# Values and float64 words loaded in pairs, combine weights turned by float32r products, four more unread products

## The chip, the cores and the metric

The kernel runs on one core of a Trainium2 chip. The metric is the device time of one execution in microseconds; a lower one is better. Several executions are timed, and one more is recorded by the hardware profiler, which gives the rows below.

## What is computed

Three layers follow one another on 4608 tokens of 512 channels, in float32, and the last one has weights in float64.

```python
# 1. attention inside chunks of 64 positions, 8 batches x 8 heads, head width 64
scores = q_c @ k_c.T / 8;  attn = softmax(scores);  x = attn @ v_c
# 2. soft mixture of 8 experts, 4 slots each (32 slots)
logits = x @ phi                                   # 4608 x 32
d = softmax over tokens(logits);  slot_in = d.T @ x  # 32 x 512
h = relu(slot_in[e] @ w1[e]);  slot_out[e] = h @ w2[e]
c = softmax over slots(logits);  y = c @ slot_out    # "combine weights" c
# 3. SoLU layer, w_in and w_out are float64
h = y @ w_in;  s = h * softmax(h);  out = layernorm(s) * g_ln @ w_out
```

## The kernel before, in words

The tokens are 36 tiles of 128. A first loop takes one tile per step: scores S (line 254), their row maximum (L263), the subtraction (L269), exp (L275), a transpose of the attention weights (L405), the product with the values (L280), the division by the row sums, a transpose of the result (L414) and its slot logits. Softmax over tokens is kept running over blocks of four tiles.

Beside each step the loop converts one chunk of the float64 weights of the last layer. A chunk is 128 x 256 words of 64 bits, loaded as pairs of 32-bit words into a tile `raw`; ScalarE makes a mask value of the high words (`sq`, L204) and shifts the low words (`t`, L208), VectorE takes high words twice (`u`, L211; `a`, L221), GpSimd puts the pieces together. Step i converts chunk i - 2 and issues, at the name `raw`, the load of chunk i + 2. The 32 chunks have four `raw` tiles. Values come one tile at a time into `vall` (three places, L180), queries and keys into three buffers (L175), and at the name `W` the next of 64 expert weight tiles of 512 KB is loaded if the table `PACE` allows it and one of 24 ring buffers is free (L128).

The order of everything is written by hand. `STEP` holds four lines, one for step i mod 4 = 0 to 3, and each name in a line issues its instructions in that order. `FIRST` orders the first loads. After step 33 `ORDER` names every operation once; a program checks that what an operation needs has gone before. Engines work through their own instructions in order. All loads go out on SyncE, in order too; each waits for its buffer and for one of eight places in the queue, and the place is free when the load eight before it has landed.

When the loop ends, buffers that it no longer needs are given to the weight loads (`homes`, `own`): the `raw` tiles, the query buffers, the values and so on. After the last tile a short chain makes the slot inputs: logits of the last block, maximum over tokens (`mnl`, `mb`), exp, the slot sums (`sl`, L681), their scaling (`siT`). Then TensorE takes the expert products in the order of the weight tiles (L933, L970, L984; last the tiles `wc48` to `wc63`). Between them stand the turns of the combine weights, `ct0` to `ct8`: for four tiles of tokens the weights are split into a high and a low float32r part (`cc`), transposed by TensorE (`combine_t`, L916) and copied to `c4T`. The names `id0` to `id3` are products of the identity with itself into PSUM that nobody reads (L643). From 191 us on the last layer runs, bound to products L1307 and L1389.

Of the kernel before, what the change touches and what calls it, by code (L numbers as in the profile page):

```python
# [9 lines left out]
F32 = mybir.dt.float32  # L10
F32R = mybir.dt.float32r
# [9 lines left out]
NB = 9  # L21
RING = 24
NRAW = 32
# [6 lines left out]
S a m t x xT u mT qk rz PT mx v xTe sub PTe W rc add mul raw exp xm mn d sq de  # L30
S a x u v m qk rz sl mx t W raw rc z xT sub xTe PT PTe add xm acc mul sq exp
m t S u a x qk rz xT mx W sub xTe PT rc acc v PTe add LT xm mul sq raw exp lte
t m a S x u L tm v mx xT add qk PT lall rz mul xTe sub rc raw PTe W sq xm exp
"""
# [8 lines left out]
GATE = dict()  # L43
FIRST = "raw0 qk0 qk1 v0 qk2 v1 cs raw1 g phi raw2 raw3"
ORDER = """
cq1 cq2 cq3 cq4 cq5 cq6 cq7 S34 loadw xT31 PT33 xtev31 x32 mx34 rz32 LT31 sub34 ev32 own_c S35 ptev33 lte7 mx35 exp34
sub350 PT34 x33 ptev34 xT32 exp350 L7 rz33 xtev32 own_q sub351 x34 ev33 exp351 PT350 id0 rz34 ptev0 xT33 PT351 LT32 lall7
tm7 x350 ptev1 ev34 x351 xtev33 xT34 LT33 id1 xtev34 own_v rz35 rc35 ev350 ev351 LT34 id2 xT350 px lte8 xT351 xtev350 xtev351
L8 own_p LT35 tm8 mT8 lte83 Ls mn8 L83 lall83 hz1 mnl own_t mb lall8 cm0 id3 d7 d8 mc de7 al sl71 de8 sl70 own_x hz0 z8
sl80 zacc8 sl81 zt acc80 acc81 zr si0 si1 siT open2 cm1 w1_000 cme w1_001 cz0 rl00 w1_010 cms2 cms6 px2 cms3 ht00 he00  # L50
# [17 lines left out]
def soft_moe_kernel(ctx: ExitStack, tc, qkT, v1, w12, w64, phi, g_ln, cst, out):  # L68
# [95 lines left out]
    for i in range(3):  # L164
        nc.vector.memset(qk[i][:, 0, :], 0.0)
        nc.gpsimd.memset(qk[i][:, 2, :], 0.0)
    vall = cvb.tile([128, 3, 520], F32, name="vall")
    XT = cvb.tile([128, 4, 4, 128], F32, name="xt_b")
# [9 lines left out]
    def load_v(t):  # L178
        if t < NT:
            gated("v", nc.sync.dma_start(out=vall[:, t % 3, :], in_=v1[t]))  # L180

    raw_t = {}

    def load_raw(c):
        if c < NRAW:
            raw_t[c] = cvp.tile([128, 256, 2], U32, tag="raw", name="raw", bufs=4)
            gated("raw", nc.sync.dma_start(out=raw_t[c].rearrange("p n t -> p (n t)"), in_=w64[c].bitcast(U32)))

# [88 lines left out]
    def x_mm(i, x, pt, g):  # L277
        for a in range(2):
            for c in range(2):
                nc.tensor.matmul(  # L280
                    x[ts(c, 64), a, ts(g, 65)],
                    pt[ts(a, 64), ts(c, 64)],
                    vall[ts(a, 64), i % 3, ts(2 * g + c, 65)],
                    start=True, stop=True, tile_position=(64 * a, 64 * c),
                )
# [183 lines left out]
    def step_ops(i):  # L469
# [20 lines left out]
        def W():  # L490
# [4 lines left out]
            u=(cvc, lambda: cv_u(c)), m=(cvc, lambda: cv_m(c)), a=(cvc, lambda: cv_a(c)), add=(cvc, lambda: cv_s(c)),  # L495
            mul=(cvc, lambda: cv_w(c)), raw=(cvc, lambda: load_raw(c + 4)),
            sq=(True, lambda: cv_sq(cstep.get(i + 1, NRAW))), t=(True, lambda: cv_t(cstep.get(i + 1, NRAW))),
# [75 lines left out]

    op("x32")(lambda: (pe_x(n - 3), load_v(n)))
    op("x33", "ptev33 ev32")(lambda: pe_x(n - 2))
# [70 lines left out]
    op("id1", "LT33 id0")(lambda: idle(lt_t[last][:, 3, :], 2))  # L646
    op("id2", "LT34 id1")(lambda: idle(lt_t[last][:, 3, :], 2))
    op("id3", "cm0 mnl ev34 id2")(lambda: idle(sx[:, 0, 256:384], 2))

# [109 lines left out]

    def raw_pair():  # L760
        return [
            cvp.tile([128, 256, 2], U32, tag="raw", name="w_raw", bufs=4).rearrange("p n t -> p (n t)").bitcast(F32)
            for _ in range(2)
        ]

# [7 lines left out]
    homes = dict(  # L773
        raw0=raw_pair, raw1=lambda: raw_pair(),
        conv=lambda: [conv.bitcast(F32).rearrange("p (k a) n -> p k (a n)", k=2)],
        v=lambda: [va[:, 0:1024].rearrange("p (a b) -> p a b", a=2)],
        pt=pt_pair, p=p_pair,
        xt0=lambda: [XT[:, 0:2].rearrange("p t g n -> p t (g n)")], xt1=lambda: [XT[:, 2:4].rearrange("p t g n -> p t (g n)")],
# [14 lines left out]
    op("own_q", "S35 own_c")(lambda: own("qk2"))  # L793
    op("own_v", "x34 x351 own_q")(lambda: own("v", "pt"))
    op("own_p", "own_v x351 PT34")(lambda: own("p"))
# [82 lines left out]

    e1 = ps2 = soT = cz = mx = late = c4T = e3c = ps3 = None
    op("open2", "siT")(open_2)  # L880
# [27 lines left out]
    def combine_t(b):  # L908
        cc = cc_t[b].bitcast(F32)
        if ps3 is None:  # L910
            t = ps2.tile([128, 4, 128], F32, tag="c", name="c_ps")
        else:
            t = ps3.tile([128, 4, 128], F32, tag="uhT_ps", name="c_ps", bufs=1)
        T["c", b] = t
        for k in range(4):
            nc.tensor.transpose(t[:, k, :], cc[:, k].rearrange("p r s -> p (r s)"), ident)  # L916

# [173 lines left out]
    def open_late():  # L1091
        nonlocal late, c4T, e3c
# [401 lines left out]
```

## Time and profile before

| | us |
|---|---|
| runs | 408.98, 413.80, 414.86 (median 413.8) |
| profiled execution | 411.12 |
| its span, first to last instruction | 409.3 |
| TensorE busy / VectorE / ScalarE / GpSimd in the span | 388.1 / 312.7 / 224.5 / 200.3 |
| moved by DMA | 99.2 MB, mean 242 GB/s |

Busy time of TensorE is modelled, so that 95% does not say that it works at its peak. What bounds a stretch is read from what its engines waited for, and from the GB/s of that stretch. [...]

### The profile page before, as it was taken

The page shows a single profiled execution, that of the slowest core. Times are in us where ns is not written, and L with a number is a line of the kernel's source. Part 1 is how long each engine was busy: PE and PEld are TensorE (multiplying, and loading weights), DVE is VectorE, ACT ScalarE, POOL GpSimd, SP SyncE. Part 2 cuts the span into 40 slices and gives each one's busy share as a digit, 9 for nine tenths or more (in the row PEclk, how much of TensorE's full clock was granted, in tenths as well). Part 3 has the DMA queues.
Part 4 walks back from the last instruction along what each step waited for, and adds up shares of the span by engine and source line. Part 5 has one row for each costly group of instructions (what it writes and reads, how often), then busy time and mean ns, then how long its engine had stood idle before and what let it go on. Part 6 is the DMA issues. An engine that isn't in the chain of part 4 may idle for free. (4 is left out here: it accounts for less than half of the span.)

```text
span 409.3 us, 10399 instructions
## 1 busy us (share of the span) xinstructions
PE 388.1 (95%) x3953; PEld 223.0 (54%) x3953; DVE 312.7 (76%) x777; ACT 224.5 (55%) x471; POOL 200.3 (49%) x198
## 2 busy tenths in 40 slices
PE   3998998999999899989999999999999999999996
PEld 2776776877787652345544444444444444444445
DVE  2688888889887447683898989998888888888840
ACT  2477877777785412232557775555455555455521
POOL 1477776677778228240013345555454444544430
PEclk9999999999999989999999999999999999999999
DMA  7999999999999999994055767777556666587671
GB/s 264 307 377 400 389 370 389 395 398 388 400 381 386 398 382 385 408 408 134 2 95 134 132 137 158 157 157 158 135 132 153 147 134 132 134 148 152 131 156 51
DMA packets 106337, 99.20 MB, mean 242 GB/s; under 512 B 78640, under 2 KB 79280, under 8 KB 106288
## 3 DMA queue, kind: packets, MB, share of 16 engines
q1 hardware_dynamic: 106288, 98.55, 78.0%
q8 instruction: 31, 0.51, 0.5%
q14 instruction: 18, 0.15, 0.1%
HBM read 70.60 MB, written 9.44 MB: 196 GB/s over the span
## 5 line engine op out<-in xcount | busy, mean ns | idle before, releaser
L1190 POOL TENSOR_SCALAR uh<-u,sc 128x1024 f16<-128x1024 f32 (+1 forms) x35 | 66.1, 1889 | 50.5 <-issue 37.6
L1389 PEld LDWEIGHTS <-uhT 128*128 128x128 f16 x560 | 52.2, 98 | 68.4 <-issue 8.9
L1389 PE MATMUL o_ps<-xb,uhT 128*128 128x512 f16 x280 | 66.6, 380 | 0.7 <-DMA uhT<-uh 0.7
L1389 PE MATMUL o_ps<-xb,ulT 128*128 128x512 f16 x280 | 66.3, 379 | 0.1
L1389 PE MATMUL o_ps<-wo,uhT 128*128 128x512 f16 x280 | 66.1, 379 | 0.0
L1318 ACT ACTIVATE e<-h_ps,nm 128x1024 f32<-128x1024 f32 x34 | 37.8, 1113 | 44.9 <-DVE nm L1312 44.9
L1206 ACT ACTIVATE e<-u,nmean 128x1024 f32<-128x1024 f32 x35 | 40.1, 1147 | 28.5 <-DVE nmean L1205 28.4
L254 PE MATMUL s_ps<-qk 128*64 128x128 f32 x576 | 42.4, 292 | 9.2 <-DMA qk<-in_qkT 6.7
L1356 POOL TENSOR_TENSOR a<-a,mhalf 128x1 f32<-128x1 f32 x36 | 21.8, 606 | 56.3 <-DVE a L1373 43.4
L1312 DVE TENSOR_REDUCE nm<-h_ps 128x1 f32<-128x1024 f32 x34 | 41.5, 1221 | 10.2 <-PE h_ps L1307 10.2
L1181 DVE SCALAR_TENSOR_TENSOR u<-h_ps,e 128x1024 f32<-128x1024 f32 x35 | 42.8, 1224 | 6.6 <-ACT e L1318 6.6
L1389 PEld LDWEIGHTS <-ulT 128*128 128x128 f16 x280 | 27.2, 98 | 33.5 <-DMA ulT<-ul 0.6
L1366 DVE SCALAR_TENSOR_TENSOR ul<-u,sc,uh 128x1024 f16<-128x1024 f32 x35 | 45.4, 1296 | 0.0
L254 PEld LDWEIGHTS s_ps<-qk 128*64 128x64 f32 x576 | 33.4, 145 | 16.3 <-issue 10.0
L263 DVE TENSOR_REDUCE mx<-s_ps 128x8 f32<-128x512 f32 x36 | 24.7, 686 | 13.0 <-PE s_ps L254 12.8
L396 ACT ACTIVATE xt_b<-xt_ps 128x512 f32<-128x512 f32 (+1 forms) x37 | 21.6, 586 | 16.3 <-PE xt_ps L414 15.3
L217 POOL TENSOR_SCALAR conv<-conv 128x256 f32<-128x256 f32 x16 | 17.4, 1090 | 23.7 <-ACT conv L204 23.1
L1407 ACT ACTIVATE ob<-o_ps,a 128x512 f32<-128x512 f32 x35 | 23.8, 680 | 9.4 <-PE o_ps L1389 8.0
L1307 PE MATMUL h_ps<-s,c4T 128*128 128x512 f32 x68 | 27.5, 488 | 0.0
L280 PE MATMUL x_ps<-vall,pt 64*64 64x65 f32 x1088 | 24.4, 227 | 1.9 <-issue 0.8
L275 ACT ACTIVATE p<-p 128x512 f32<-128x512 f32 x35 | 21.8, 621 | 7.0 <-DVE p L269 7.0
L217 POOL TENSOR_SCALAR conv<-conv,g_sb 128x256 f32<-128x256 f32 x16 | 19.0, 1185 | 12.2 <-ACT conv L204 12.2
(234 smaller groups left out, 643.2 us busy)
## 6 DMA issues: line engine op xcount, KB each, us to landing
w<-in_w SPq DMA_DIRECT2D x48, 512.0 KB, 7.6
qk<-in_qkT SPq DMA_DIRECT2D x72, 256.0 KB, 5.8
vall<-in_v SPq DMA_DIRECT2D x36, 260.0 KB, 5.9
out<-ob SPq DMA_DIRECT2D x35, 256.0 KB, 2.1
raw<-in_w SPq DMA_DIRECT2D x32, 256.0 KB, 5.9
qk<-in_w SPq DMA_DIRECT2D x3, 512.0 KB, 8.6
w_raw<-in_w SPq DMA_DIRECT2D x4, 256.0 KB, 6.8
vall<-in_w SPq DMA_DIRECT2D x2, 512.0 KB, 8.6
```

The costliest lines, as they stand in the source:

```text
L217: nc.gpsimd.tensor_scalar(out=m, in0=m, scalar1=1.265625 * 2.0 ** -30, scalar2=g, op0=ALU.is_ge, op1=ALU.mult)
L254: nc.tensor.matmul(s[ts(c, 64), ts(g, 128)], b[:, 1, ts(2 * g + c, 64)], b[:, 0:3:2, ts(2 * g + c, 64)], start=True, stop=True, tile_posit ...
L263: mark("mx", nc.vector.tensor_reduce(out=mx, in_=s, axis=AX.X, op=ALU.max))
L280: nc.tensor.matmul(x[ts(c, 64), a, ts(g, 65)], pt[ts(a, 64), ts(c, 64)], vall[ts(a, 64), i % 3, ts(2 * g + c, 65)], start=True, stop=True, ...
L1181: nc.vector.scalar_tensor_tensor(out=u, in0=d["h"], scalar=1.0, in1=e, op0=ALU.mult, op1=ALU.mult, accum_out=zz[:, 1:2])
L1190: nc.gpsimd.tensor_scalar(out=uh[:, 0:n], in0=u[:, 0:n], scalar1=d["sc"][:, 1:2], scalar2=1.0, op0=ALU.mult, op1=ALU.mult)
L1206: nc.scalar.activation(out=d["e"], in_=d["u"], func=AF.Square, bias=nmean, scale=1.0, accum_out=d["zz"][:, 2:3])
L1307: nc.tensor.matmul(h[:, ts(n, 512)], c4T[:, i, :], s4[n], start=True, stop=True)
L1312: nc.vector.tensor_reduce(out=nm, in_=st[i]["h"], axis=AX.X, op=ALU.max, negate=True)
L1318: nc.scalar.activation(out=d["e"], in_=d["h"], func=AF.Exp, bias=d["nm"], scale=1.0, accum_out=d["zz"][:, 0:1])
L1366: nc.vector.scalar_tensor_tensor(out=ul, in0=d["u"], scalar=d["sc"][:, 1:2], in1=d["uh"], op0=ALU.mult, op1=ALU.subtract)
L1389: nc.tensor.matmul(d["o"], lt(n % 8), w(n % 8), start=(n == 0), stop=(n == 23))
```

## The change

1. *Loads in pairs.* Values are stored in the input as two tiles per row of 1040 elements, and one load brings both into two of now four places of `vall`. Words of two chunks come with one load into one of two double tiles `raw`; the load is issued at the name `raw` of the odd chunks' steps, for chunks c + 3 and c + 4, and that name stands further ahead in its two lines of `STEP`. The values of tile 35 come with those of tile 34, so `x32` loads none.
2. *First loads.* `FIRST` begins with the constants (`cs`, with the identity in it), and the first raw load stands behind the first values.
3. *Space.* The ring has 23 places; `vall` is longer by 520 elements, and with a tile `spare` of 512 its new part makes one more home for a weight tile (`vx`).
4. *Turns.* `combine_t` multiplies by a float32r constant `pick` = (0, I, 0) of which 256 columns are read: (I, 0) for the first of a pair, (0, I) for the second, both accumulated into the same 256 columns of PSUM. `pick` is filled by VectorE at `late`.
5. *Unread products.* `id4` (one product), `id5` (one) and `id6` (two) come in `ORDER` between the end of the last tile's transposes and the maximum over tokens.

```diff
-RING = 24
+RING = 23
 # STEP, lines of steps i mod 4 = 1 and 3
-S a x u v m qk rz sl mx t W raw rc z xT sub xTe PT PTe add xm acc mul sq exp
+S a x u raw v m qk rz sl mx t W rc z xT sub xTe PT PTe add xm acc mul sq exp
-t m a S x u L tm v mx xT add qk PT lall rz mul xTe sub rc raw PTe W sq xm exp
+t m a S x u raw L tm v mx xT add qk PT lall rz mul xTe sub rc PTe W sq xm exp
-FIRST = "raw0 qk0 qk1 v0 qk2 v1 cs raw1 g phi raw2 raw3"
+FIRST = "cs qk0 qk1 v0 raw0 qk2 g phi raw2"
 # ORDER
-... id2 xT350 px lte8 xT351 xtev350 xtev351
-L8 own_p LT35 tm8 mT8 lte83 Ls mn8 L83 lall83 hz1 mnl own_t mb lall8 cm0 id3 ...
+... id2 xT350 px lte8 xT351 id4 xtev350 xtev351
+L8 own_p LT35 id5 tm8 mT8 lte83 Ls mn8 L83 id6 lall83 hz1 mnl own_t mb lall8 cm0 id3 ...
-    vall = cvb.tile([128, 3, 520], F32, name="vall")
+    vall = cvb.tile([128, 4, 520], F32, name="vall")
+    spare = cvb.tile([128, 512], F32, name="spare")
-        if t < NT:
-            gated("v", nc.sync.dma_start(out=vall[:, t % 3, :], in_=v1[t]))
+        if t < NT and t % 2 == 0:
+            gated("v", nc.sync.dma_start(out=vall[:, t % 4:t % 4 + 2, :].rearrange("p a d -> p (a d)"), in_=v1[t // 2]))
-        if c < NRAW:
-            raw_t[c] = cvp.tile([128, 256, 2], U32, tag="raw", name="raw", bufs=4)
-            gated("raw", nc.sync.dma_start(out=raw_t[c].rearrange("p n t -> p (n t)"), in_=w64[c].bitcast(U32)))
+        if c < NRAW and c % 2 == 0:
+            raw = cvp.tile([128, 2, 256, 2], U32, tag="raw", name="raw", bufs=2)
+            raw_t[c], raw_t[c + 1] = raw[:, 0], raw[:, 1]
+            gated("raw", nc.sync.dma_start(out=raw.rearrange("p k n t -> p (k n t)"), in_=w64[c // 2].bitcast(U32)))
-            mul=(cvc, lambda: cv_w(c)), raw=(cvc, lambda: load_raw(c + 4)),
+            mul=(cvc, lambda: cv_w(c)), raw=(cvc, lambda: load_raw(c + 3)),
-    op("x32")(lambda: (pe_x(n - 3), load_v(n)))
+    op("x32")(lambda: pe_x(n - 3))
+    op("id4", "xT351 ev34 id2")(lambda: idle(sx[:, 0, 256:384], 1))
+    op("id5", "LT35 id4")(lambda: idle(sx[:, 0, 256:384], 1))
+    op("id6", "L83 lte8 id5")(lambda: idle(lt_t[last][:, 0, :], 2))
+        vx=lambda: [va[:, 1536:2048], spare],
-            nc.tensor.transpose(t[:, k, :], cc[:, k].rearrange("p r s -> p (r s)"), ident)
+            nc.tensor.matmul(
+                t[:, k - k % 2:k - k % 2 + 2, :], cc[:, k].rearrange("p r s -> p (r s)"), pick[:, 1 - k % 2:3 - k % 2, :],
+                start=(k % 2 == 0), stop=(k % 2 == 1),
+            )
+        pick = late.tile([128, 3, 128], F32R, name="pick")
+        nc.vector.memset(pick.bitcast(F32)[:, 0:3:2, :], 0.0)
+        nc.vector.tensor_copy(out=pick[:, 1, :], in_=ident)
-        "v1": v1.reshape(36, 128, 520),
+        "v1": v1.reshape(18, 2, 128, 520).transpose(0, 2, 1, 3).reshape(18, 128, 1040),
```

The change moves instructions in three places. The first is SyncE at the start; `qk_111` to `qk_113` are the three buffers of queries and keys. Before:

```order
1 L187 DMA raw<-in_w 128x512
2 L175 DMA qk_111<-in_qkT 64x1024 x2
3 L175 DMA qk_112<-in_qkT 64x1024 x2
4 L180 DMA vall<-in_v 128x520
5 L175 DMA qk_113<-in_qkT 64x1024 x2
6 L180 DMA vall<-in_v 128x520
7 L239 DMA cs<-in_cst 128x257
8 L187 DMA raw<-in_w 128x512
```

And with the change:

```order
1 L241 DMA cs<-in_cst 128x257
2 L176 DMA qk_111<-in_qkT 64x1024 x2
3 L176 DMA qk_112<-in_qkT 64x1024 x2
4 L181 DMA vall<-in_v 128x1040
5 L189 DMA raw<-in_w 128x1024
6 L176 DMA qk_113<-in_qkT 64x1024 x2
```

The constants went from the tenth load to the first, the first raw load from the first to the seventh, and the third queries stand behind more bytes.

The second place is SyncE in the loop, two steps of it; `DMAHW0` to `DMAHW7` are the eight places of the queue. Before:

```order
43 L180 DMA vall<-in_v 128x520 [waits DMAHW2_49,PE_49]
44 L187 DMA raw<-in_w 128x512 [waits DMAHW3_49,DVE_49,Activation_49]
45 L180 DMA vall<-in_v 128x520 [waits DMAHW4_49,PE_49]
46 L175 DMA qk_112<-in_qkT 64x1024 [waits DMAHW5_49]
47 L175 DMA qk_112<-in_qkT 64x1024 [waits DMAHW6_49]
48 L187 DMA raw<-in_w 128x512 [waits DMAHW7_49,DVE_49,Activation_49]
49 L175 DMA qk_113<-in_qkT 64x1024 [waits DMAHW0_49,PE_49]
50 L175 DMA qk_113<-in_qkT 64x1024 [waits DMAHW1_49]
```

With the change:

```order
36 L189 DMA raw<-in_w 128x1024 [waits DMAHW3_49,DVE_49,Activation_49]
37 L181 DMA vall<-in_v 128x1040 [waits DMAHW4_49,PE_49]
38 L176 DMA qk_112<-in_qkT 64x1024 [waits DMAHW5_49]
39 L176 DMA qk_112<-in_qkT 64x1024 [waits DMAHW6_49]
40 L176 DMA qk_113<-in_qkT 64x1024 [waits DMAHW7_49,PE_49]
41 L176 DMA qk_113<-in_qkT 64x1024 [waits DMAHW0_49]
42 L128 DMA w<-in_w 128x1024 [waits DMAHW1_49]
```

Two steps hold six loads besides the weights where they held eight, and values and queries follow directly behind the wait of the raw load for VectorE and ScalarE.

The third place is TensorE from the last transposes of the attention to the slot sums (`L_ps`, `mT_ps`, `mb_ps` are logits, transposed maxima and the spread maximum). Before:

```order
210 L627 MATMUL xt_ps<-cs,xl_149 128x128 x2
211 L349 MATMUL L_ps<-cs,ltb 128x32 x3
212 L309 MATMUL lt_ps<-xt_b,phi_sb 32x128 x4
213 L717 MATMUL mT_ps<-cs,tm 32x128
214 L735 MATMUL s_ps<-ltb,cs 32x128
215 L349 MATMUL L_ps<-cs,ltb 128x32
216 L371 MATMUL mb_ps<-cs,mn 128x32
217 L821 MATMUL cm_ps<-csum,mean_l 128x256
218 L643 MATMUL s_ps<-cs 128x128 x2
```

With the change:

```order
210 L629 MATMUL xt_ps<-cs,xl_145 128x128 x2
211 L645 MATMUL s_ps<-cs 128x128
212 L351 MATMUL L_ps<-cs,ltb 128x32 x3
213 L311 MATMUL lt_ps<-xt_b,phi_sb 32x128 x4
214 L645 MATMUL s_ps<-cs 128x128
215 L722 MATMUL mT_ps<-cs,tm 32x128
216 L740 MATMUL s_ps<-ltb,cs 32x128
217 L351 MATMUL L_ps<-cs,ltb 128x32
218 L645 MATMUL lt_ps<-cs 128x128 x2
219 L373 MATMUL mb_ps<-cs,mn 128x32
```

The rows of L645 at 211, 214 and 218 are new; the last two of them stand directly ahead of the product `mb_ps`.

## Rows read from the trace of the kernel before

**Rows 1.** The page: span, TensorE's busy time, DMA share in 40 slices.
```profile
span 409.3 us, 10399 instructions
PE 388.1 (95%) x3953; PEld 223.0 (54%) x3953; DVE 312.7 (76%) x777; ACT 224.5 (55%) x471; POOL 200.3 (49%) x198
DMA  7999999999999999994055767777556666587671
```

**Rows 2.** Busy time by stage: stretch, its length, engines, clock, DMA share, GB/s.
```profile
10.00:18.00 8.00, 7.28 (x82) 5.77 (x79) 4.64 (x10) 2.95 (x8) 2.55 (x3) 1.00 0.87 286
30.00:120.00 90.00, 85.83 (x1685) 67.29 (x1683) 77.21 (x195) 66.70 (x176) 65.74 (x76) 1.00 1.03 392
130.00:150.00 20.00, 18.25 (x247) 12.90 (x244) 7.91 (x27) 8.21 (x25) 5.55 (x5) 0.91 1.04 401
160.00:186.00 26.00, 24.36 (x269) 9.74 (x269) 18.75 (x36) 7.73 (x17) 9.47 (x10) 1.00 1.03 409
188.00:190.00 2.00, 1.51 (x53) 1.18 (x42) 0.42 (x1) 0.42 (x2) 0.00 (x0) 1.00 0.15 37
```

**Rows 3.** The chain that ended last: start, us, what.
```profile
243.23 0.45 PE h_ps L1307 x2
...
385.35 15.55 PE o_ps L1389 x72
```

**Rows 4.** DMA issues of the page: count, KB each, median us to landing.
```profile
w<-in_w SPq DMA_DIRECT2D x48, 512.0 KB, 7.6
...
raw<-in_w SPq DMA_DIRECT2D x32, 256.0 KB, 5.9
```

**Rows 5.** Timeline of VectorE: row maxima of steps 4, 27, 31, 32.
```profile
21.11 0.68 DVE L263 TENSOR_REDUCE mx<-s_ps 128x8 f32<-128x512 f32 x1
...
103.88 0.68 DVE L263 TENSOR_REDUCE mx<-s_ps 128x8 f32<-128x512 f32 x1
...
117.64 0.68 DVE L263 TENSOR_REDUCE mx<-s_ps 128x8 f32<-128x512 f32 x1
...
120.40 0.68 DVE L263 TENSOR_REDUCE mx<-s_ps 128x8 f32<-128x512 f32 x1
```

**Rows 6.** Timeline: last read of chunk 11, first read of chunk 14.
```profile
52.75 0.48 DVE L211 TENSOR_SCALAR conv<-raw 128x256 int32<-128x256 int32 x1
...
60.15 0.44 ACT L208 ACTIVATE conv<-raw 128x256 int32<-128x256 uint32 x1
```

**Rows 7.** Timeline of the start: ScalarE's first conversion, TensorE's first transposes.
```profile
9.55 0.42 ACT L208 ACTIVATE conv<-raw 128x256 int32<-128x256 uint32 x1
...
11.77 1.08 PE L405 MATMUL pt_ps<-cs,p 128*128 128x128 f32 x4 [0.72 <-DMA cs<-in_cst]
```

**Rows 8.** Tile 35's value product; by stage, unread products L643, slot sums L681.
```profile
136.59 0.70 PE L280 MATMUL x_ps<-vall,ptl 64*64 64x65 f32 x32 [0.35 <-DMA vall<-in_v]
...
138.00:139.00 1.00, 0.71 (x4) 0.52 (x4) 1.00 1.06 391
...
143.80:147.20 3.40, 1.94 (x16) 0.60 (x16) 0.50 1.05 399
...
147.20:150.00 2.80, 1.07 (x16) 0.42 (x16) 1.00 1.03 398
```

**Rows 9.** Timeline of TensorE: first use of the last weight tile.
```profile
190.57 0.29 PE L984 MATMUL h_ps<-w_pt,hTb 128*4 128x128 f32 x2
```

**Rows 10.** One turn in the timeline; weight loads of L916 and L1307, min/median/max ns.
```profile
172.98 0.66 PE L916 MATMUL c_ps<-cs,cc 128*128 128x128 f32 x4
...
L916 PEld LDWEIGHTS c_ps<-cs,cc x36: 137/140/143, 170.6 to 193.9; 128*128 128x128 f32 x36
...
L1307 PEld LDWEIGHTS h_ps<-s,c4T x68: 187/190/190, 205.8 to 384.7; 128*128 128x128 f32 x68
```

**Rows 11.** Timeline of VectorE behind the place of the new fill.
```profile
170.21 0.29 DVE L1068 TENSOR_REDUCE isw<-wm_ps 128x1 f32<-128x128 f32 x1 [2.12 <-PE wm_ps L1065]
```

More of the change, by code (lines that the diff above doesn't have):

```diff
@@ L47 @@
 sub350 PT34 x33 ptev34 xT32 exp350 L7 rz33 xtev32 own_q sub351 x34 ev33 exp351 PT350 id0 rz34 ptev0 xT33 PT351 LT32 lall7
-tm7 x350 ptev1 ev34 x351 xtev33 xT34 LT33 id1 xtev34 own_v rz35 rc35 ev350 ev351 LT34 id2 xT350 px lte8 xT351 xtev350 xtev351
-L8 own_p LT35 tm8 mT8 lte83 Ls mn8 L83 lall83 hz1 mnl own_t mb lall8 cm0 id3 d7 d8 mc de7 al sl71 de8 sl70 own_x hz0 z8
+tm7 x350 ptev1 ev34 x351 xtev33 xT34 LT33 id1 xtev34 own_v rz35 rc35 ev350 ev351 LT34 id2 xT350 px lte8 xT351 id4 xtev350 xtev351
+L8 own_p LT35 id5 tm8 mT8 lte83 Ls mn8 L83 id6 lall83 hz1 mnl own_t mb lall8 cm0 id3 d7 d8 mc de7 al sl71 de8 sl70 own_x hz0 z8
 sl80 zacc8 sl81 zt acc80 acc81 zr si0 si1 siT open2 cm1 w1_000 cme w1_001 cz0 rl00 w1_010 cms2 cms6 px2 cms3 ht00 he00
@@ L282, in x_mm @@
                     pt[ts(a, 64), ts(c, 64)],
-                    vall[ts(a, 64), i % 3, ts(2 * g + c, 65)],
+                    vall[ts(a, 64), i % 4, ts(2 * g + c, 65)],
                     start=True, stop=True, tile_position=(64 * a, 64 * c),
@@ L758, in soft_moe_kernel, with raw_home @@
     va = vall.rearrange("p a b -> p (a b)")
[L760 to L764, printed above, removed]
+    def raw_home():
+        raw = cvp.tile([128, 2, 256, 2], U32, tag="raw", name="w_raw", bufs=2)
+        return [raw.rearrange("p k n t -> p k (n t)").bitcast(F32)]
     def p_pair():
@@ L773, in soft_moe_kernel @@
     homes = dict(
-        raw0=raw_pair, raw1=lambda: raw_pair(),
+        raw0=raw_home, raw1=lambda: raw_home(),
         conv=lambda: [conv.bitcast(F32).rearrange("p (k a) n -> p k (a n)", k=2)],
         v=lambda: [va[:, 0:1024].rearrange("p (a b) -> p a b", a=2)],
+        vx=lambda: [va[:, 1536:2048], spare],
         pt=pt_pair, p=p_pair,
@@ L793, in soft_moe_kernel @@
     op("own_q", "S35 own_c")(lambda: own("qk2"))
-    op("own_v", "x34 x351 own_q")(lambda: own("v", "pt"))
+    op("own_v", "x34 x351 own_q")(lambda: own("v", "vx", "pt"))
     op("own_p", "own_v x351 PT34")(lambda: own("p"))
@@ L877, in open_2 @@
         mx = e1.tile([128, 9], F32, name="wmx")
-    e1 = ps2 = soT = cz = mx = late = c4T = e3c = ps3 = None
+    e1 = ps2 = soT = cz = mx = late = c4T = e3c = ps3 = pick = None
     op("open2", "siT")(open_2)
@@ L908, in combine_t @@
     def combine_t(b):
-        cc = cc_t[b].bitcast(F32)
+        cc = cc_t[b]
         if ps3 is None:
@@ L1091, in open_late @@
     def open_late():
-        nonlocal late, c4T, e3c
+        nonlocal late, c4T, e3c, pick
         tmp.close()
@@ L1472 @@
         "qkT": qkT,
-        "v1": v1.reshape(36, 128, 520),
+        "v1": v1.reshape(18, 2, 128, 520).transpose(0, 2, 1, 3).reshape(18, 128, 1040),
         "w12": np.stack(w12),
         "w64": np.concatenate([
-            bits64(inputs["moe2_w_in"]).reshape(4, 128, 4, 256).transpose(0, 2, 1, 3).reshape(16, 128, 256),
-            bits64(inputs["moe2_w_out"]).reshape(8, 128, 2, 256).transpose(0, 2, 1, 3).reshape(16, 128, 256),
+            bits64(inputs["moe2_w_in"]).reshape(4, 128, 2, 512).transpose(0, 2, 1, 3).reshape(8, 128, 512),
+            bits64(inputs["moe2_w_out"]).reshape(8, 128, 512),
         ]),
```

## The prediction

> **What bounds the kernel now.** I read the page first, then busy time by stage, then the chain of waits, then the timelines of the places that the change touches. The page [rows 1] shows a span of 409.3 us and DMA engines that are full in every slice from the second to the eighteenth, up to about 185 us, and far from full after it. The table by stage [rows 2] says how fast they are when full: 392 GB/s in the attention loop (30 to 120 us), 409 GB/s while only expert weights come in (160 to 186 us). The chain [rows 3] ends in TensorE: from 241 us to 406 us nothing but output products follow one another, and the diff touches none of those lines. Whatever the change is worth must show before that, as an earlier start of an unchanged tail of some 219 us (from the last weights at 190 us on).
>
> Before 190 us two chains run side by side. One is the transfer stream. The other is computation: attention loop, softmax over tokens, then the expert products, which take the weights in the order in which they arrive. The last bytes are in by about 189 us, since 188 to 190 us moves only 37 GB/s [rows 2]; the last weight tile is first used at 190.57 us [rows 9]. So the weights come some 1.6 us before they are needed: computation is the bound there by a hair, and if it moves forward by more than the stream's own gain plus 1.6 us, the stream becomes the bound.
>
> Inside the loop the two are just as close. The row maximum of step 4 starts at 21.11 us and that of step 32 at 120.40 us [rows 5], so four steps take 14.18 us on average. The same four steps from 103.88 to 117.64 us take 13.76 us. I take 13.76 us as what the engines need when no transfer is late.
>
> **The change part by part, in microseconds of the end of the run.**
>
> *Paired loads.* 36 loads of values become 18 and 32 loads of words become 16, with the same 18.0 MB in pieces of 4160 and 4096 bytes where they were 2080 and 2048. How fast pieces of half a row go is not shown alone. Upper bound: all of the difference between 392 and 409 GB/s in the loop comes from them; over the 110 us in which they are read that is 110 x (1 - 392/409) = 4.6. Lower bound: nothing, if that difference is the queries' and keys' (64 partitions to a transfer). The nearest row is 130 to 150 us [rows 2]: 401 GB/s in a mix in which 14 loads of 256 KB, pieces of 2048 bytes too, are up to 46% of the bytes. 1/401 = 0.54/409 + 0.46/r gives r = 392 GB/s for the half pieces, so 18.0 MB would take 45.9 where it takes 44.0 at 409. I take 1.9 of transfer time saved. The loop cannot pass all of it on: it cannot go under its own 13.76 per four steps, so over the seven groups between steps 4 and 32 at most 7 x 0.42 = 2.9 is to be had, and a part of that excess is not the transfers'. I take **-1.5**. The trace says why the number of transfers as such should not count: the DMA share is 1.03 in the loop [rows 2], so whatever a transfer costs besides its bytes is spent beside the next ones.
>
> *Raw words two chunks at a time.* The load of chunks c+3 and c+4 can be issued only when the vector engine has read chunk c, and ScalarE's first read of c+3 stands early in the second step after it. In the trace the shortest such distance that I found runs from 53.24 us (52.75 + 0.49) to 60.15 us [rows 6]: 6.9. A 256 KB load lands 5.9 after its issue, a 512 KB load 7.6 [rows 4]. So a pair can be up to 0.7 late, and ScalarE, which works in order, would hold the exponentials behind it. I take 0, since a late pair delays the loop only where the transfer queue runs dry meanwhile, and that is rival C. On SyncE the values and the next queries are now queued behind this wait; both are needed two to three steps later, and each of them waits there for one of eight places in the queue as well.
>
> *The first loads.* The identity now comes first. The first transposes waited 0.72 for it at 11.77 us [rows 7]; that is the most to be won. Against it, the first raw load is twice as long and stands behind five loads, while the conversion that reads it (9.55 us) stands ahead of the second exponential on ScalarE, and the third queries come behind 644 KB more, 2.3 at the 286 GB/s of that stretch, of which the 0.7 was spare. Bounds -0.7 and +1.6; I take **-0.3**, nearer the row that shows a wait.
>
> *The last values.* Tile 35's values now come with tile 34's. TensorE waited 0.35 for them at 136.59 us [rows 8]: **-0.3**, between 0 and -0.4.
>
> *Four unread products.* [...] Two unread products take 0.71 with their pipeline's end, so at most 0.35 each [rows 8]; two of the four stand alone in waits for ScalarE or VectorE, the last two stand ahead of the product that spreads the maximum, and can delay it by up to 0.4. If the clock holds: -0.87 + 0.3 = -0.6. If not: +0.3. I take holding as somewhat likelier and enter **-0.4**. [...]
>
> *Turning the combine weights.* 36 transposes of 128 columns become 36 float32r products of 256 columns. Four transposes take 0.66 [rows 10]. Two float32r products of 512 columns take 0.45 [rows 3], so one of 256 takes some 0.11, which is a transpose's pace as well. The weight load of such a product takes 190 ns against 140 [rows 10]. If only the first of a turn shows, +0.05 a turn; if they cannot overlap the products, 4 x (0.19 - 0.11) = +0.32 a turn. Eight of the nine turns stand in TensorE's order before 190 us, where it is busy 24.36 of 26 [rows 2]: +0.4 to +2.6, and -0.4 if the float32r product has the shorter end. I take **+0.3**. On VectorE, a fill and a copy for the new right-hand side stand ahead of a 2.12 wait [rows 11]; they are some 0.5 and cost nothing.
>
> *Space.* The ring of weight buffers has 23 places and not 24, and the longer value buffer gives one more at the loop's end. The number of tiles that can be in place before the experts start stays the same: 0, and the stream after the loop is one tile (512 KB) longer, 1.3 that the loop no longer carries.
>
> Sum: -1.5 - 0.3 - 0.3 - 0.4 + 0.3 = **-2.2**. The profiled execution took 411.1 us (409.3 of span and 1.8 around it), so 408.9. The three runs shown are 409.0, 413.8 and 414.9, with the profiled one a mean of 412.2; against that mean the change gives 410.0. I predict **409.8** for the median.
>
> **Rivals.** *A, the forecast:* 407 to 412. Chance 0.57.
>
> *B, it is given back.* The loop is held by its own engines and gives 0.5, the values 0.3, the clock still falls (+0.3) and the turns cost 1.0, between their ends: +0.5 against the profiled execution, 411.6, or 412.7 by the mean. For it: four steps at 13.76 with transfers on time show how little is left. Chance 0.23.
>
> *C, slower.* A raw pair lands later than its 6.9, every second step from the sixth on, 14 times. The place is ScalarE's conversion, the price the lateness that the queue does not hide. It decides from a landing time of about 7 us, and 7.6 is what a 512 KB load takes now. If all of 0.7 passed through, 14 x 0.7 = 9.8, less the 0.7 that the terms outside the loop bring: +9.1, 420 to 421. Against it: the engines move bytes meanwhile, and a loop that starts later also issues later, which shortens the queue. Chance 0.08, half of it over 2%.
>
> *D, the whole excess.* The loop runs at 13.76 throughout (-2.9), the start gives 0.7, the values 0.3, the clock 0.9, the turns nothing: -4.8, 406.3, or 407.4 by the mean. The stream nearly allows it: 1.9 of its own, the start's 0.7 and the 1.6 in hand are 4.2, and the last 0.6 would be waits for weights, so 407 to 408. [...] Chance 0.12.
>
> That a run of 4160 bytes is moved as two packets would take the values' half of the 1.9 away; it lies inside A and B.
>
> **The numbers.** The range holds A, B and most of D, and the runs' own spread: 404.5 to 414.5. About 2% is what a measurement of this kernel can tell from no change: under 405.5 or over 422. Faster 0.09 (part of D, and runs that fall low), slower 0.04 (half of C), within 0.87.
>
> **What would show it.** Loop: the row maxima of steps 4 and 32 about 97.8 apart, GB/s from 30 to 120 us at 396 or more. Raw: no idle time of ScalarE that ends with a raw load; several of 0.5 and up would be C. Clock: no stretch at 0.50 between 140 and 150 us, and slot sums of 1.07 twice. Turns: four products within 0.75. End: the first use of the last weight tile near 188.4 us and everything after it as long as now. I am wrong if the time before 190 us moves by over 5, or if the tail changes at all.

## The result, and the profile after

The change is a little slower, where a gain of 2.2 us was forecast. Its runs have a median of 412.0 us (19 runs, 408.23 to 415.54), those of the kernel before beside them one of 411.25 (19 runs, 407.49 to 416.72); the ratio is 1.0054, with a 95% interval of 1.0028 to 1.0080. The ratio leaves out slow executions, over 1.5% above the fastest of their kernel (four of the 19 before and two of the 19 after), which is why it is further from 1 than that of the two medians, 1.0018. Run again as a control among the experiments it gave 1.0062 (1.0033 to 1.0092). 412.0 lies in the range 404.5 to 414.5 and within 2%, but on the other side of zero.

The two profiled executions say the opposite: 409.87 after, 411.12 before. One execution of the kernel before differs from another by up to 9 us, so a loss of some 2 us (2.2 by the first ratio, 2.5 by the control's) can't be read off one pair of traces. What can be read off is each stage, as it went in that execution. After, the page and the busy time by stage (columns as in [rows 1, 2]):

```profile
span 408.1 us, 10354 instructions
...
PEclk9999999999999999999999999999999999999999
DMA  7999999999989999993056667778558675576661
GB/s 246 392 403 408 399 357 413 384 379 400 381 320 372 405 393 410 408 406 102 2 103 136 124 145 144 171 157 157 133 134 150 151 129 135 134 149 151 133 157 51
```

```profile
10.00:18.00 8.00, 7.19 (x118) 5.61 (x115) 5.48 (x12) 4.34 (x11) 3.91 (x5) 1.00 1.03 410
30.00:120.00 90.00, 85.56 (x1679) 66.79 (x1675) 76.27 (x192) 65.63 (x176) 64.30 (x75) 1.00 1.00 384
130.00:150.00 20.00, 19.50 (x270) 13.62 (x270) 9.58 (x29) 7.93 (x25) 6.10 (x6) 1.00 1.03 402
160.00:186.00 26.00, 24.08 (x259) 10.53 (x251) 18.45 (x41) 7.13 (x16) 7.51 (x9) 1.00 1.05 402
...
188.00:190.00 2.00, 1.24 (x38) 1.08 (x41) 0.17 (x1) 0.28 (x1) 0.00 (x0) 1.00 0.01 4
```

The loop moved 384 GB/s from 30 to 120 us, where 396 or more had been forecast and 392 were before. The page shows a slice of 320 GB/s, where the page before has nothing under 370 from the fourth slice to the eighteenth:

```profile
GB/s 264 307 377 400 389 370 389 395 398 388 400 381 386 398 382 385 408 408 134 2 95 134 132 137 158 157 157 158 135 132 153 147 134 132 134 148 152 131 156 51
```

The timelines of the change at the places of [rows 5, 8, 9, 10]: row maxima of steps 4 and 32, tile 35's values, the first expert product, a turn, the first use of the last weight tile:

```profile
20.00 0.68 DVE L265 TENSOR_REDUCE mx<-s_ps 128x8 f32<-128x512 f32 x1
...
120.23 0.68 DVE L265 TENSOR_REDUCE mx<-s_ps 128x8 f32<-128x512 f32 x1
...
135.65 0.29 PE L282 MATMUL x_ps<-vall,ptl 64*64 64x65 f32 x4
...
148.44 0.61 PE L940 MATMUL h_ps<-w,xl 128*4 128x512 f32 x4
...
172.44 0.74 PE L920 MATMUL c_ps<-pick,cc 128*128 128x256 f32 x4 [0.25 <-ACT c4T L398]
...
189.47 0.28 PE L991 MATMUL h_ps<-w_pt,hTb 128*4 128x128 f32 x2
```

The first expert product before:

```profile
150.47 0.61 PE L933 MATMUL h_ps<-w,xl 128*4 128x512 f32 x4
```

And the slot sums (L686) after the change, busy time of TensorE and its weight loads in two stretches, with the granted clock (a share of full speed), the DMA share and GB/s:

```profile
144.00:145.20 1.20, 1.07 (x16) 0.42 (x16) 1.00 1.06 393
145.60:148.00 2.40, 1.07 (x16) 0.42 (x16) 1.00 1.06 393
```

Step 4 comes 1.1 us earlier, and all of it but 0.2 is gone at step 32: the loop between them takes 100.23 us and not 99.29. After it everything is as hoped: no wait for tile 35's values, slot sums of 1.07 twice at a clock of 1.00, so that the experts start 2.0 us earlier than before. Then the expert stage gives back 0.9: from its first product to the first use of the last weight tile 41.03 us, before 40.10. The tail is as long as it was (218.6 and 218.8).

TensorE waited 1.1 us for queries before and 2.1 after; in the control, whose profiled execution (411.92 us) is at its median, 3.0. The rows are before, after and the control, from 20 to 122 us: what waited, what it waited for, us in total, times, longest.

```profile
PE s_ps L254 <- DMA qk<-in_qkT: 1.1, 2, 0.8
...
PE s_ps L256 <- DMA qk<-in_qkT: 2.1, 3, 0.9
...
PE s_ps L256 <- DMA qk<-in_qkT: 3.0, 4, 1.1
```

What else changed on the way shows in the waits of SyncE's queue (same stretch and columns). Before:

```profile
SPq L175 <- DMA w<-in_w: 6.2, 9, 1.4
SPq L180 <- PE L_ps L354: 3.8, 4, 1.4
SPq L187 <- ACT rz L302: 3.5, 7, 1.2
SPq L128 <- DMA w<-in_w: 3.0, 4, 0.8
SPq L175 <- DMA qk<-in_qkT: 2.3, 10, 0.3
```

And after (L189 loads words, L181 values, L176 queries and keys):

```profile
SPq L189 <- DVE conv L213: 22.8, 13, 2.4
SPq L181 <- PE L_ps L356: 11.0, 7, 3.7
SPq L176 <- PE s_ps L256: 6.1, 8, 1.5
```

Before, SyncE waited mostly for a place in the queue, which a landing transfer frees: 22.3 us, against 17.0 for engines that still read a buffer (sums of the same view). After, it waits 3.2 for places and 43.3 for engines. Eight loads were under way, from issue to landing, in 76% of the time from 30 to 122 us before, and in 16% after. SyncE's waits have moved from places in the queue to buffers.

### The profile page after: what moved, and what is told of

The parts are those of the page before. It is cut to its first block, busy times and chain, and to the rows that moved or that the text cites. A ratio compares the mean times of both kernels' runs of the same rounds, so it can differ in the third digit from the quotient of the medians.

```text
span 408.1 us, 10354 instructions
## 1 busy us (share of the span) xinstructions
PE 387.4 (95%) x3961; PEld 223.5 (55%) x3961; DVE 312.7 (77%) x779; ACT 224.1 (55%) x471; POOL 199.8 (49%) x198
## 5 line engine op out<-in xcount | busy, mean ns | idle before, releaser
L1399 PEld LDWEIGHTS <-ulT 128*128 128x128 f16 x280 | 27.2, 98 | 33.5 <-DMA ulT<-ul 0.7
L219 POOL TENSOR_SCALAR conv<-conv 128x256 f32<-128x256 f32 x16 | 17.6, 1100 | 22.1 <-ACT conv L206 22.1
```

The costliest lines, as they stand in the source:

```text
L219: nc.gpsimd.tensor_scalar(out=m, in0=m, scalar1=1.265625 * 2.0 ** -30, scalar2=g, op0=ALU.is_ge, op1=ALU.mult)
L1399: nc.tensor.matmul(d["o"], lt(n % 8), w(n % 8), start=(n == 0), stop=(n == 23))
```

## The experiments

Ratios are to the kernel before on the same chip, with 95% intervals.

**The parts alone.** Products, turns and first loads:

```diff
 # e1_products
+... xT351 id4 ...  LT35 id5 ...  L83 id6 ...
 # e2_turns
-            nc.tensor.transpose(t[:, k, :], ..., ident)
+            nc.tensor.matmul(t[:, k - k % 2:k - k % 2 + 2, :], ..., pick[:, 1 - k % 2:3 - k % 2, :], ...)
 # e6_first
-FIRST = "raw0 qk0 qk1 v0 qk2 v1 cs raw1 g phi raw2 raw3"
+FIRST = "cs qk0 qk1 v0 raw0 qk2 v1 raw1 g phi raw2 raw3"
```

> The kernel before with the four unread products alone (id4, id5, id6 at their places in the order). Theory T3, the clock: in the profiled execution of before the granted clock fell to 0.50 for 3.4 us and the slot sums took 1.94 in place of 1.07; with the products the profile shows 1.00 from 140 to 150 us, sums of 1.07 twice, and siT 0.6 to 0.9 us earlier against the last row maximum, so a ratio of 0.998 to 0.9985. Theory T3', the fall of the clock is not in every execution of before: then the products cost their 0.3 us and the ratio is 1.000 to 1.001. Neither gives more than 1.001; a ratio above it would say that the products themselves are late for the spread of the maximum.

> The kernel before with the float32r turns alone (pick, (I,0) and (0,I), 256 columns). Theory T1, the turns carry the excess of the change: eight turns before 190 us take 0.73 and not 0.66, +0.6 us on TensorE, and their weight loads and the wait before the next expert product add as much again; ratio 1.003 to 1.006, and the first use of the last weight tile moves back by 1.2 to 2.4 us against the start of the experts. Rival T2, the loads carry it: then the turns are worth only their own rows, +0.1 to +0.6 us, ratio 1.000 to 1.0015.

> The kernel before with the order of the first loads alone (constants first, first words behind the first values). Theory F, the start carries the excess of the change: row maximum of step 4 no earlier than before (21.1 us) although the first transposes need not wait, ratio 1.002 to 1.005. Rival Q, SyncE's waits for the two double tiles carry it: ratio 0.998 to 1.001.

Measured: products 0.9990 (0.9949 to 1.0031), turns 1.0006 (0.9966 to 1.0046), first loads 1.0003 (0.9964 to 1.0041). None of them shows the loss. The intervals of turns and first loads reach up to 1.004, so these ratios alone don't exclude T1 (the turns carry it) or F (the start does). In e6 the row maximum of step 4 came at 21.22 us, no earlier than before, as F said, but the ratio is where Q (SyncE's waits carry it) had it. The products' ratio doesn't tell T3 from T3'. The turns' stage is exact, though: first expert product 150.11, last weight tile

```profile
190.86 0.29 PE L987 MATMUL h_ps<-w_pt,hTb 128*4 128x128 f32 x2
```

so 40.75 us, +0.65, about half of T1's lower end of 1.2.

Values alone, words alone, and both with the new first loads but without turns and products:

```diff
 # e4_values (ring 23, four places)
+ if t % 2 == 0: dma_start(out=vall[:, t % 4:t % 4 + 2, :], in_=v1[t // 2])
 # e5_raw (ring 24)
+FIRST = "raw0 qk0 qk1 v0 qk2 v1 cs g phi raw2"
+ if c % 2 == 0: raw = cvp.tile([128, 2, 256, 2], ..., bufs=2); dma_start(out=raw, in_=w64[c // 2])
 # e3_loads: the diff of the change without pick, id4, id5, id6
```

> The kernel before with the paired values alone (520 KB each, four places, ring of 23). Theory Q, SyncE's queue: in the change SyncE stood 22.8 us before the word loads, waiting for VectorE to finish with the tile that they overwrite, and 11.0 us before the value loads, waiting for TensorE; eight loads were under way in 16% of the time from 30 to 122 us, where it was 76% before. With values alone only the second wait is there: SyncE waits about 10 us at the values, eight are under way in 45 to 65% of the time, ratio 1.000 to 1.002. Rival P, the longer packets by themselves make the queries land later (7.3 us after issue in the change, 6.6 before): then half of the excess is here, ratio 1.002 to 1.004, with eight under way as often as before.

> The kernel before with the paired words alone (512 KB, two double tiles, issued early in the odd steps). Theory Q: SyncE waits 18 to 25 us at the word loads, eight are under way in less than 40% of the time, the loop from step 4 to step 32 is 0.5 to 2 us longer than with the values alone, ratio 1.002 to 1.005. Rival P: eight under way as before, queries land 7 us after issue, ratio 1.002 to 1.004.

> The change without its turns and without its four products: paired values, paired words, the new order of the first loads and the ring of 23 places. Theory T2, the loads carry the excess: the loop from the row maximum of step 4 to that of step 32 takes 100 us or more where before took 99.29, because queries and keys stand behind 512 KB words and 520 KB values; ratio 1.002 to 1.006. Rival T1, the turns carry it: the loads give back what the forecast said, ratio 0.995 to 0.999, loop 98 to 99 us.

Measured: values 0.9955 (0.9918 to 0.9992), words 0.9988 (0.9957 to 1.0018), all loads 1.0050 (1.0007 to 1.0093). So the loads carry the loss, but only values and words together; neither alone shows one. (e3 has the new first loads as well, which show nothing in e6.) Rival P, the longer packets by themselves, falls with both. Theory Q had not expected this either: it gave 1.000 to 1.002 for the values and 1.002 to 1.005 for the words, and for the words 18 to 25 us of waiting and eight loads under way in less than 40% of the time. They were 10.6 us and 57%:

```profile
SPq L188 <- DVE conv L212: 10.6, 10, 1.5
```

SyncE's waits for engines are 18.9 us in sum with the values, 29.2 with the words, 48.1 with both.

**One part taken out of the change**, and the change as a control:

```diff
 # e8_noturns
+            nc.tensor.transpose(t[:, k, :], ..., ident)
 # e7_oldfirst
+FIRST = "raw0 qk0 qk1 v0 qk2 cs g phi raw2"
```

> The change with the old turns (transposes of 128 columns), all else as in the change, whose ratio to the kernel before was 1.0054. Theory T1, the turns carry the excess: ratio 0.999 to 1.002, and the last weight tile is used 1.2 us or more nearer to the start of the experts. Rival T2, the loads carry it: 1.004 to 1.005, and the stage from siT to the last weight tile is shorter by only 0.6 us than in the change.

> The change with the old order of its first loads (first words first, constants behind the third queries). Theory F: the ratio to the kernel before falls from 1.0054 to 0.997 to 1.001. Rival Q: it stays, 1.003 to 1.006, and SyncE waits about 20 us at the word loads as in the change.

> The change itself, unaltered, beside the others on the same chip as the control: theories Q and F both expect its first ratio, 1.003 to 1.008. Rival N, that the ratio of 1.0054 belonged to the runs it came from and not to the kernel: 0.997 to 1.002.

Measured: without turns 1.0016 (0.9974 to 1.0057), old first loads 1.0037 (0.9996 to 1.0078), control 1.0062 (1.0033 to 1.0092). The loss is the kernel's (rival N falls). e7 is nearer to Q than to F, though its interval excludes neither. e8 can't be told from either end of its expectation; its expert stage took 40.37 us, 0.66 less than the change's, which is the turns' 0.65 once more.

**What the word tiles cost.** A third double tile; the same with six places for values; the same with the old turns; and the word load back at its old place:

```diff
 # e9_raw3            e10_raw3_v6: also RING = 21, vall 6 x 520     e17_raw3_noturns: e9 with the transposes
-RING = 23
+RING = 22
-            raw = cvp.tile([128, 2, 256, 2], U32, tag="raw", name="raw", bufs=2)
+            raw = cvp.tile([128, 2, 256, 2], U32, tag="raw", name="raw", bufs=3)
 # e15_raw_later, odd lines of STEP
-S a x u raw v m qk rz sl mx t W rc ...
+S a x u v m qk rz sl mx t W raw rc ...
```

> The change with three double tiles for the words in place of two, and a ring of 22 in place of 23, so that a word load no longer overwrites a tile which VectorE still reads. Theory Q: SyncE's wait of 22.8 us at the word loads goes under 3 us, eight loads are under way in over 50% of the time, GB/s from 30 to 120 us at 392 or more where the change had 384, and the ratio falls from 1.0054 to 0.996 to 1.001. Rival P, packets: the wait goes but the time stays, ratio 1.003 to 1.006. Rival T1, turns: 1.002 to 1.006 too.

> As the run with three double tiles, and with six places for values in place of four, ring of 21. Theory Q: SyncE's 11 us before the value loads go too, eight loads are under way in over 70% of the time, as before the change; ratio 0.994 to 1.000, and the loop from step 4 to step 32 is 97.5 to 99 us. If the two stages are bound by the computation alone, the loop is no shorter than with three double tiles alone. Rival P: ratio 1.003 to 1.006.

> The change with three double tiles for the words, a ring of 22, and the old turns (transposes of 128 columns): all parts of the change that may pay, without the two that cost. From the first use of a weight to that of the last tile 40.1 to 40.4 us where every kernel with the new turns and a shorter ring took 41.0; loop 98.5 to 99.5 us; ratio 0.995 to 0.999, 0.0015 below the run with three double tiles and the new turns (0.9986). If it is not below that, the turns cost nothing that lasts.

> The change, with the word loads back at their old place in the odd steps, behind values, queries and expert weights. Theory Q: SyncE no longer stands long before a word load with the other loads behind it (under 10 us where it was 22.8), ratio 0.998 to 1.003, if the words still come in time. Theory D: nothing that matters changes, 1.004 to 1.008. Rival C, the words are now late: ScalarE idles for them, 0.5 us or more at a time, ratio 1.008 to 1.02.

Measured: third tile 0.9986 (0.9952 to 1.0020), with six places 0.9978 (0.9948 to 1.0008), with old turns 0.9995 (0.9958 to 1.0032), later word load 1.0216 (1.0155 to 1.0278). The interval of the third tile lies wholly under the control's: the loss goes with one more tile. The ring, shorter by one place, took nothing out of the loop: 18 or 19 weight loads are issued before step 32 in the change, the control and the three kernels with a third tile. Its SyncE waits and its loop:

```profile
SPq L181 <- PE L_ps L356: 16.3, 7, 3.5
SPq L176 <- PE s_ps L256: 7.5, 9, 1.6
SPq L181 <- PE x_ps L282: 5.0, 7, 1.3
...
30.00:120.00 90.00, 85.95 (x1695) 67.09 (x1687) 77.07 (x195) 66.58 (x177) 65.61 (x76) 1.00 1.01 392
```

The wait for VectorE at the words is gone, and 392 GB/s are back, as theory Q said (385 in e17). One number of Q was wrong: eight loads were under way in only 26% of the time, not over 50%, as SyncE now stands at the values; nor was it over 70% with six places, but 32%. With six places it stands at the queries (27.2 us before L176), which means that it is ahead there, and the loop is no shorter (98.68 and 98.70 us): late queries don't bound either. e17 is not below e9, so the turns' 0.65 us can't be seen in whole runs.

In e17 SyncE waits nearly as long for engines as in the change, 39.0 us against 6.1 for places, with eight loads under way in 14% of the time, and no loss shows:

```profile
SPq L181 <- PE L_ps L356: 18.6, 7, 3.5
SPq L176 <- PE s_ps L256: 8.5, 10, 1.9
SPq L181 <- PE x_ps L282: 8.1, 7, 2.2
```

So it isn't the sum of SyncE's waits that costs. What went with the third tile is the place of the waits, from the words to the values and queries, and the late queries: TensorE waits for none of them in e9, e10 and e17.

The later word load shows the other side, in ScalarE's waits:

```profile
ACT conv L210 <- DMA raw<-in_w: 17.6, 12, 2.7
```

In the change this is 0.3 in all. Q's 0.998 to 1.003 held only if the words came in time; they are late, as rival C said. So the words need their early place, and it is there that SyncE stands before them; in e15 it stands 32.8 us before the values instead.

**Size of the loads.** Two loads for each pair, into the same tiles and at the same place:

```diff
 # e18_words_two
+            for h in range(2):
+                dma_start(out=raw[:, h], in_=w64[c // 2][:, 256 * h:256 * h + 256])
 # e19_both_two, also
+            for h in range(2):
+                dma_start(out=vall[:, t % 4 + h, :], in_=v1[t // 2][:, 520 * h:520 * h + 520])
```

> The change, with each pair of word chunks brought by two loads of 256 KB one behind the other (pieces of 2048 bytes), into the same double tile and at the same place in the order. Theory D, the size of the load: TensorE's waits for its program between steps 4 and 32 fall from 2.2 to 4.3 us to under 1.5, queries land under 7 us after issue, ratio 0.998 to 1.003. Theory Q, the two double tiles and SyncE's wait before each: the wait is as long as in the change (about 20 us in sum), so are the program's and the queries' waits (4 to 6 us in sum); ratio 1.004 to 1.008. If the longer pieces were worth what the forecast took for them, the ratio rises by 0.002 to 1.008 to 1.010.

> As the run with the words in two loads, and the values in two loads of 260 KB too, into the same four places. Theory D: the rest of the excess goes, 0.996 to 1.001, loop of 98.5 to 100 us. Theory Q: 1.004 to 1.010, no lower than with the words alone; the loop is 100 us or longer.

Measured: words in two loads 1.0111 (1.0056 to 1.0166), values too 1.0130 (1.0086 to 1.0173). Theory D falls: the smaller loads are worse. Against the control, joining the loads of both is worth about 0.7% (1.0130 less 1.0062), some 2.8 us; the two intervals overlap slightly, and leave the difference anything from 0.6 to 5.0 us. So joining the loads does pay, and the tiles which came with it cost more than it pays. But theory Q missed as well: it expected SyncE to wait as long as in the change. In e19, the slower of the two, the wait at the words is less than half of the change's:

```profile
SPq L191 <- DVE conv L215: 9.8, 12, 1.3
```

SyncE's waits for engines are 31.2 us in sum in e18 and 24.0 in e19, and eight loads are under way in 45 and 62% of the time. Here, too, the loss doesn't follow the sum of the waits.

Cutting the weight loads instead told nothing about D, since it changed the transfers themselves:

```diff
 # e14_change_split (the change), e16_before_split (the kernel before)
+                for h in range(2 if m < 19 else 1):
+                    dma_start(out=t[0][64 * h:64 * h + 64], in_=w12[m][64 * h:64 * h + 64])
```

> The change, with each expert weight load of the loop (tiles 0 to 18, 512 KB) cut into two of 64 partitions, 256 KB, pieces as long as before. Theory D, depth: with larger loads the same eight places hold more bytes (2.47 MB on average from 30 to 122 us, 2.30 before the change), so that queries and the 16 KB loads of TensorE's program queue longer and TensorE waits for them; cut in two, 1.9 to 2.1 MB are under way, queries land 6.0 to 6.6 us after issue (7.2 in the change), and the ratio falls from 1.006 to 0.997 to 1.002. Theory Q, SyncE's waits before the word and value loads leave the stream too little under way: with smaller loads there is still less, ratio 1.006 to 1.015, and GB/s from 30 to 120 us under 384.

> The kernel before with the expert weight loads of the loop cut in two of 256 KB. Theory D: less is under way (1.8 to 2.0 MB where it was 2.30), queries land earlier than 6.6 us, TensorE waits less for its program; ratio 0.994 to 0.999. If eight places then hold too little to keep the engines full, GB/s from 30 to 120 us falls under 385 and the ratio is 1.000 to 1.010. Theory Q expects the second.

Measured: 1.1042 (1.0991 to 1.1093) and 1.0953 (1.0890 to 1.1016), both far outside every expectation, with eight loads under way in 80 to 85% of the time. The loop of e14:

```profile
30.00:120.00 90.00, 72.32 (x1266) 57.58 (x1262) 57.15 (x141) 48.82 (x128) 45.38 (x54) 0.87 1.03 294
```

The DMA engines are full (1.03) and move 294 GB/s. More on that below.

**A better version.** Paired values and the products, all else as before:

> The kernel before with the two parts that cost nothing alone: paired values (0.9955 alone) and the four unread products (0.999 alone); words, first loads and turns as before. If the parts add up, 0.993 to 0.997, 408 to 409.5 us, and the profile shows clock 1.00 from 130 to 150 us and the loop in 98.5 to 99.5 us. If the computation alone bounds the run once the loads are on time, the second part adds what the first has not used, 0.9945 to 0.997. Rival N, the parts' small ratios are spread of the runs: 0.998 to 1.002.

```diff
 # e11_values_products: the lines of e4_values and of e1_products
```

Measured 0.9966 (0.9931 to 1.0000); values alone gave 0.9955. The two can't be told apart, and the parts do not add up visibly. Both beat the change, whose interval begins at 1.0028; values alone is the smallest edit that beats the kernel before.

## Why the prediction failed, step by step

I take TensorE's time between the row maxima of steps 4 and 32 apart, in all profiles: time in which it isn't idle; idle time at places of its program that lie 256 of its records or a multiple apart ("program", below); idle time that ends with a load of queries; other idle time. Means of the kernels with the same loads, one profiled execution each, in us:

| loads | kernels | loop | not idle | program | queries | other |
|---|---|---|---|---|---|---|
| as before | before, e1, e2, e6 | 99.7 | 94.4 | 1.0 | 1.2 | 3.2 |
| values paired | e4, e11 | 98.8 | 94.2 | 0.7 | 2.1 | 1.8 |
| words paired | e5 | 100.4 | 94.4 | 2.0 | 1.1 | 3.0 |
| the change's | after, e3, e7, e8, e13 | 101.8 | 95.2 | 3.0 | 1.9 | 1.8 |
| with a third tile | e9, e10, e17 | 99.1 | 94.5 | 2.5 | 0.0 | 2.2 |

Against the kernels with a third tile, the change's loop is 2.7 us longer: 1.9 of it is the wait for queries, 0.7 time not idle, 0.5 program, less 0.4 of other waits. The sizes are rough. In e3 and e7 the clock fell inside the loop (below), and their profiled executions lie 1.9 and 3.5 us above the medians of their kernels; without these two the mean loop of the change's loads is 100.6, and that of the control, whose execution is at its median, 102.1.

**The step that failed** is the words two chunks at a time, "I take 0". It priced the landing of a pair against ScalarE's need, and rightly: pairs were hardly ever late (0.3 us in all). What it named and gave no price is its last sentence, that values and queries are queued behind the wait. Before, the load of chunk c + 4 overwrites chunk c, one tile at a time. In pairs, c + 3 must also wait until c has been read, so the first chunk of a pair has lost a step of its lead. To keep it in time the load stands early in its step, where VectorE has not yet read c: 1.8 us of standing each, 13 times, with the values and the next queries behind it. With single values such waits (10.6 us in e5) cost nothing that the runs show; with the values paired too, the kernel is slower than before, and a third tile, with which SyncE no longer waits for VectorE before the words, removes the loss. The loop became 2.1 us longer in the mean of the table where 1.5 less was forecast: 3.6 of the 4.7 by which the forecast is off (2.2 forecast as a gain, 2.5 lost by the control), and 2.4 without e3 and e7.

**Paired loads, -1.5.** The size of the gross gain was about right: 1.9 forecast; the paired values alone give 1.8 in whole runs (0.9955), which holds the last values' part too, and joining both 2.8, roughly, by e19 against the control. The floor was wrong: I took 13.76 us for four steps from the best group, so 96.3 for seven. No profile has the loop under 98.5 (e1), and in the three in which no query was late it took 98.7, 98.7 and 99.9. So no more than 0.8 below the traced 99.29 was ever seen.

**First loads, -0.3.** Not to be seen: 1.0003, with an interval of some 1.6 us either way. **Last values, -0.3.** Rather too small: from the row maximum of step 35 to the first expert product e11 takes 17.58 us, e1, which differs in the paired values and their ring, 18.31. Tile 35's value product waits 0.68 in e1 and 1.18 in e2, where it waited 0.35 before; the view names no load in these two, so that it is the values is likely and not shown.

**Unread products, -0.4.** The 0.87 from which it is worked out is 1.94 for the slot sums at a clock of 0.50 less 1.07 at 1.00 [rows 8]. That four products would hold the clock was my estimate, and no trace of before shows it. The runs agree with it: in twelve profiles with them the clock was 1.00 there, in the six without it fell twice (before, 0.83 from 140 to 150 us; e3, 0.67 from 145 to 150); e14 and e16, with their stretched loops, are left out. The runs' mean clocks say the same: 0.999 or more in all 24 runs of e1 and e11, but 0.996 or less in 14 of the 35 runs of the kernel before beside e1. As it falls in some executions alone, the mean gain is less than the one traced.

**Turns, +0.3.** 0.65, and always 0.65. A turn takes 0.74 and not 0.66, within "+0.05 to +0.32", and eight of them are on the path. **Space, 0.** It was +0.27 (40.37 us for the stage in e4 and e8, 40.10 before): with the paired values and their ring, product L1051 of the change, ahead of the last tiles, waits 0.77 for ScalarE's copy of `xb`, where it waited 0.49 before (L1044). Why the copy is later isn't settled. The stream after the loop is no tile longer than before, though the prediction has it one longer: 19 weight loads are issued before step 32 in both profiles.

**The rivals.** B's time, 411.6 to 412.7, is what came, but not by its way, since the clock held and the loop grew. C's mechanism is real, as e15 shows (17.6 us of ScalarE's waits); the change escapes it by the early place, and pays there. D fell with the floor of the loop.

Open is the last link. It is shown that two double tiles together with paired values cost, and that a third tile removes the loss. That the waits before the words do it through late queries is argued: queries wait 1.9 us in the mean of the change's profiles and 0 with a third tile, but 2.1 in e4 and e11, which lose nothing. TensorE's idle times of the column "program" are longer in the nine profiles of the table with paired words, 1.4 to 4.3 us, than in those without, 0.4 to 1.5 except for one of 0.2. They are 2.5 with a third tile, where the loss is gone, so they don't carry it alone; e15, with 0.2, shows that they are no plain effect of the pairs.

## What to carry to other kernels

Look at what the issuing engine stands before, whether a place in the queue or a buffer ends the wait, and what is queued behind it. The sum alone says little: e17 stands 39.0 us for engines and shows no loss, e19 24.0 and loses 1.3%. A joined load into half as many tiles loses one unit of lead; give it one tile more, or leave it. And take a loop's floor from a run in which nothing is late, not from its best group.

## What the runs showed of the hardware

**Loads to 64 partitions.** With the weight loads cut into partitions 0 to 63 and 64 to 127 the loop moved 294 GB/s (e14) and 290 (e16) with full engines (1.03 and 1.00), where it moved 384 and 392 uncut; a piece of 4096 bytes took 241 and 175 ns (medians, 30 to 120 us), 159 uncut. The queries' loads are of 64 partitions as well, but of every second one; over half of the pieces of 4096 bytes before are theirs, with that median of 159. Why the cut loads were slower, no run shows.

**TensorE is idle at fixed places of its program.** The page counts 31 instruction loads (q8), 0.51 MB, 16 KB each. Idle time of TensorE, most of which no wait explains, stands at the same places of the program from profile to profile, 256 of its records apart or a multiple of that (products, weight loads and semaphore instructions counted), some 2.4 us after such a load began. After the change 0.24 us of it stand ahead of its record 705, 0.22 ahead of 3009, 0.66 ahead of 3522 and 0.99 ahead of 3778 (here the view names a wait for ScalarE), each 2.35 to 2.58 us after a load began; 513 records, the second distance, are one more than a multiple. In e3 it is 1.86 us at one of these places, in e5 1.97 and in e19 2.7 at the same one:

```profile
112.33 0.94 PE L467 MATMUL sl_ps<-xb,d 128*32 128x512 f32 x4 [1.86 <-issue]
```

with, from 109.5 to 112.5 us,

```profile
q1 hardware_dynamic: 346, 1.18, 100.5%
q8 instruction: 1, 0.02, 2.1%
```

That TensorE waits there for its own program I infer from these places and times; no view names it. The idle time comes to 0.2 to 4.3 us of a loop of 100, and it is one source of the differences between profiles.

**Three falls of the clock behind idle time.** Behind those 1.86 us of idle time the granted clock in e3 is 0.50 from 113 to almost 116 us, though TensorE is busy all the time:

```profile
113.00:114.00 1.00, 1.00 (x8) 0.00 (x0) 0.00 (x0) 0.00 (x0) 0.22 (x1) 0.50 1.06 407
```

It fell in the same way in e7 behind 1.97 us of waiting for queries (0.50 from 72 to 75 us), and in e19 at the 2.7 (0.50 from 113.6 to 119 us). It need not fall: behind the 1.97 us in e5 and other waits of up to 1.6 us in e15 it stayed at 1.00. TensorE's time not idle in the loop is 96.2 and 95.7 us in e3 and e7, 94.0 to 94.8 in the table's other profiles.
